# Gathered rows of an expert block asked for ahead, their transposes tied behind the queued unit, four row tiles

## The chip, the cores and the metric

The kernel runs on one core of a Trainium2 chip. The metric is the device time of one execution in microseconds (us). Of the core's engines, TensorE (PE) multiplies and transposes, VectorE (DVE) and ScalarE (ACT) copy and combine, GpSimd (POOL) issues the indirect transfers (gathers and scatters by a list of rows), and SyncE (SP) issues the plain ones. Each engine has a queue of its own and works through it in order.

## The reference

Attention with a block-wise causal mask, an MLP with a squared ReLU on its output, and a mixture of eight experts of which each token takes one:

```python
x = attention(q, k, v)                    # 4 x 8 heads x 576 x 64 -> x: 2304 tokens x 512
h = x @ w_in                              # 512 -> 2048
r = np.maximum(h, 0.0)
x = (r * r) @ w_out                       # 2048 -> 512
logits = x @ w_gate + modality_bias[modality_id]
e_idx = np.argmax(logits, axis=1)         # one of 8 experts
gate_w = softmax(logits)[arange(N), e_idx]
for e in range(8):
    mask = e_idx == e
    h = np.maximum(x[mask] @ w1[e], 0.0)  # 512 -> 1024
    out[mask] = gate_w[mask, None] * (h @ w2[e])
```

## The kernel before, in words

The tokens are worked in nine blocks of 256 (`BT`). Attention of later tokens runs interleaved with the MLP of earlier ones; the last MLP block, number 8, runs with no attention beside it (L873 to L886). An MLP or expert block is a list of *units* (`ffn_units`, L468): a unit f multiplies the block's transposed input, split in a high and a low part, by 128 columns of the first weight (twelve matmuls, L493 to L495, called U here), ScalarE and VectorE make gh and gl of the result (L506 to L512), and then the second matmuls of the unit before are done (L483 to L485, six for a block of 256 rows, nine for 352). An MLP block has 16 units, an expert block eight.

After each MLP block `route` (L570) writes its rows to x2d in HBM, computes the expert of each token, and scatters the token numbers into lists, one per expert (lst, L623 on POOL; the positions come from VectorE's L621). The rows of an expert block are then fetched by such a list: `load_list` (L655) loads 256 or 352 entries on SP, and `gather_block` (L666) takes the rows in tiles of 128 with an indirect DMA on POOL (L677), transposes each tile on PE (four transposes, L683, into a bank of tag s, of which there are two), and makes the high part on ScalarE (L685) and the low part on VectorE (L686).

Two experts with the most tokens after block 5 are worked as fixed blocks: the first two blocks of the first expert ("early", 256 rows each), then `blocks` (L888): its blocks of 352, 352, and four of the second expert (352, 352, 256, 256 rows). The early blocks' gathers are asked for at unit 10 of MLP block 8 (L882); the next ones at unit 6 of the second early block (L898), with the list three units before (L896), and then at unit 1 of each block for the block after it (L907). `expert_steps` (L796) splits the next expert's weights on ScalarE and VectorE (L193 to L197) beside the units; their loads (L186) are on SP. `expert_finish` (L689) scales the result and scatters it to out (L698, POOL).

What sets the order: the program is built with a scheduler that orders each engine's instructions by a simulated timeline. Code may run ahead of what was written before it, up to its data; `tc.issue_after` ties instructions behind a given one. So the place of a transpose in PE's queue is where the scheduler expects its rows to be there, and PE waits if they are not.

Of the kernel before, what the change touches and what calls it, by code (L numbers as in the profile page):

```python
# [10 lines left out]
F32 = mybir.dt.float32  # L11
# [9 lines left out]
P = 128  # L21
B, H, S, HD = 4, 8, 576, 64
N = B * S
D = H * HD
FF = 2048
E, FE = 8, 1024
KC = D // P
# [25 lines left out]
def tile_attention_mlp_moe(ctx: ExitStack, tc: tile.TileContext, qT2, kT2, v, w_in, w_out,  # L53
# [46 lines left out]
    def scratch(name):  # L100

        if late_pool:
            return late_pool[0].tile([P, D], F32, tag="xt", bufs=1, name=name)
        return apool.tile([P, S], F32, tag="p", bufs=6, name=name)[:, 0:D]
# [363 lines left out]
    def ffn_units(xh, xl, wa, wb, nf, square, finish, htag="h", bt=BT, last_blk=False):  # L468
# [18 lines left out]
        def unit(f):  # L487
# [4 lines left out]
            for k in range(KC):  # L492
                nc.tensor.matmul(hb[:, :bt], whk[:, k, :], xh[:, k, :], start=(k == 0), stop=False)  # L493
                nc.tensor.matmul(hb[:, :bt], whk[:, k, :], xl[:, k, :], start=False, stop=False)  # L494
                nc.tensor.matmul(hb[:, :bt], wlk[:, k, :], xh[:, k, :], start=False, stop=(k == KC - 1))  # L495
            if last_blk:
# [13 lines left out]
            else:  # L510
                act = nc.scalar.activation(out=gh, in_=hb[:, :bt], func=AF.Relu)  # L511
                dve = nc.vector.scalar_tensor_tensor(out=gl, in0=hb[:, :bt], scalar=0.0, in1=gh.bitcast(F32),  # L512
                                                     op0=ALU.max, op1=ALU.subtract)
            unit_ends[:] = [act, dve]
            pend.append((f, gh, gl))
# [149 lines left out]

    def gather_block(il, n):  # L666
        if n == BT:
            xh = work.tile([P, KC, BT], F32R, tag="xh", bufs=3, name="gxh")
            xl = work.tile([P, KC, BT], F32R, tag="xl", bufs=3, name="gxl")
        else:  # L670
            xh = late.tile([P, KC * LBT], F32R, tag="lxh", bufs=2, name="gxh")[:, 0:KC * n]
            xl = late.tile([P, KC * LBT], F32R, tag="lxl", bufs=2, name="gxl")[:, 0:KC * n]
            xh, xl = (x.rearrange("p (k c) -> p k c", k=KC) for x in (xh, xl))
        for t in range(-(-n // P)):
            w = min(P, n - t * P)
            g = late.tile([P, D], F32, tag="gat", bufs=3, name="gat")
            nc.gpsimd.indirect_dma_start(  # L677
                out=g[:w], out_offset=None, in_=x2d,
                in_offset=bass.IndirectOffsetOnAxis(ap=il[:w, t, 0:1], axis=0))
            tb = pbank("s", 2)  # L680
            tv = tb.rearrange("p (k q) -> p k q", k=KC)
            for k in range(KC):
                nc.tensor.transpose(tv[:, k, :w], g[:w, k * P:(k + 1) * P], ident[:w, :w])  # L683
            sl = slice(t * P, t * P + w)
            nc.scalar.copy(xh[:, :, sl], tv[:, :, :w])  # L685
            nc.vector.tensor_sub(xl[:, :, sl], tv[:, :, :w], xh[:, :, sl].bitcast(F32))  # L686
        return xh, xl
# [186 lines left out]
    early = []  # L874

    def get_early():
        for blk in range(2):
            il = load_list(rvs[0], blk, f"e{blk}")
            early.append((gather_block(il, BLKS[blk]), il))

    for f, u in enumerate(units):
        if f == NF1 // 2 + 2:  # L882
            get_early()
        if steps and f:
            steps.pop(0)()
        u()  # L886
# [4 lines left out]
    nxt = None  # L891
    for ei, ((xh, xl), il) in enumerate(early):
        for f, u in enumerate(ffn_units(xh, xl, *moe_w[0], NF2, False, expert_finish(il, BT), "pt")):
            if steps and (ei or f):
                steps.pop(0)()
            if ei and f == 3:  # L896
                lists += [load_list(rvs[0], blk, f"l0{blk}") for blk in (2, 3)]
            if ei and f == 6:  # L898
                nxt = gather_block(lists[0], BLKS[blocks[0][1]])
            u()  # L900
    lists += [load_list(loads_reg(1), blk, f"l1{blk}") for blk in ORDER]
    for gi, (i, blk) in enumerate(blocks):
        xh, xl = nxt
        n = BLKS[blk]
        units = ffn_units(xh, xl, *moe_w[i], NF2, False, expert_finish(lists[gi], n), "pt", n, gi == len(blocks) - 1)
        for f, u in enumerate(units):
            if f == 1 and gi + 1 < len(blocks):  # L907
                nxt = gather_block(lists[gi + 1], BLKS[blocks[gi + 1][1]])
            u()
# [87 lines left out]
```

## Time and profile before

| | |
|---|---|
| median of 3 runs | 892.41 us (890.43 to 898.46) |
| profiled execution | 891.78 us |
| its span, first to last instruction | 890.0 us |
| PE busy | 854.0 us (96%) |
| VectorE, ScalarE, GpSimd busy | 505.4, 400.3, 73.0 us |
| mean granted clock of PE | 0.988 |

The profile is of one execution. Busy times say what an engine did; for an engine that is nearly always busy, its waits and the stretches with a lower granted clock say where time is lost. MLP block 8 lies about from 600 to 650 us, the two early expert blocks to about 700 us, the six others after them.

### The profile page before, as it was taken

How to read it: one execution, taken by the hardware profiler on the slowest of the kernel's cores; microseconds unless marked ns; L12 is line 12 of the kernel's file. 1: busy time of each engine (PE TensorE's matmuls, PEld its weight loads, DVE VectorE, ACT ScalarE, POOL GpSimd, SP SyncE). 2: the span in 40 equal slices, each digit the busy share in tenths (PEclk: the TensorE clock that was granted, in tenths of full speed). 3: DMA queues.
4: the chain of work that ended last, by engine and by line, in shares of the span. 5: the costliest groups of instructions: out<-in, count | busy, mean ns of one | idle time of the engine just before them, and what ended most of it. 6: DMA issues, size and time to landing. Idle time of an engine off the chain costs nothing. (4 is left out here: it accounts for less than half of the span.)

```text
span 890.0 us, 16016 instructions
## 1 busy us (share of the span) xinstructions
PE 854.0 (96%) x5865; PEld 734.0 (82%) x5866; DVE 505.4 (57%) x1533; ACT 400.3 (45%) x1074; POOL 73.0 (8%) x174
## 2 busy tenths in 40 slices
PE   5799999999999999999999999999898999999997
PEld 4566778888988888888888888898787988888896
DVE  6989878968667647555837755348363312212221
ACT  6689888645555435444534434334232212112111
POOL 1000000001000000100000000100103202101011
PEclk9899999999999999999999999999998999999999
DMA  9983151221341210232211211420622101011000
GB/s 313 353 278 110 38 186 34 67 78 21 90 131 60 61 52 31 66 105 84 61 30 37 54 31 51 129 80 33 190 72 70 57 21 66 28 34 45 13 29 36
DMA packets 87922, 73.94 MB, mean 83 GB/s; under 512 B 14305, under 2 KB 75745, under 8 KB 87842
## 3 DMA queue, kind: packets, MB, share of 16 engines
q1 hardware_dynamic: 84194, 63.18, 23.9%
q0 software_dynamic: 3648, 9.72, 3.3%
q8 instruction: 47, 0.77, 0.4%
q14 instruction: 33, 0.27, 0.1%
HBM read 62.71 MB, written 10.42 MB: 82 GB/s over the span
## 5 line engine op out<-in xcount | busy, mean ns | idle before, releaser
L493 PE MATMUL h<-xh,w 128*128 128x256 f32 x512 | 149.7, 292 | 3.7 <-ACT r L506 3.7
L483 PE MATMUL acc<-w,gh 128*128 128x512 f32 x368 | 151.5, 412 | 0.4 <-ACT gh L508 0.4
L484 PE MATMUL acc<-w,gh 128*128 128x512 f32 x368 | 146.1, 397 | 0.0
L495 PE MATMUL h<-xh,w 128*128 128x256 f32 x512 | 145.9, 285 | 0.0
L494 PE MATMUL h<-xl,w 128*128 128x256 f32 x512 | 145.7, 285 | 0.0
L485 PE MATMUL acc<-w,gl 128*128 128x512 f32 x368 | 132.2, 401 | 0.0
L493 PEld LDWEIGHTS h<-xh,w 128*128 128x128 f32 x512 | 97.9, 191 | 8.8 <-ACT r L506 4.1
L506 ACT ACTIVATE r<-h 128x256 f32<-128x256 f32 x128 | 49.2, 384 | 121.2 <-PE h L495 119.2
L512 DVE SCALAR_TENSOR_TENSOR gl<-pt,gh 128x352 fp32r<-128x352 f32 (+1 forms) x56 | 26.9, 481 | 129.8 <-ACT gh L511 128.5
L494 PEld LDWEIGHTS h<-xl,w 128*128 128x128 f32 x512 | 98.0, 191 | 2.9 <-issue 0.2
L507 DVE TENSOR_TENSOR r<-r 128x256 f32<-128x256 f32 x128 | 53.9, 421 | 79.9 <-ACT r L506 79.2
L495 PEld LDWEIGHTS h<-xh,w 128*128 128x128 f32 x512 | 98.0, 191 | 0.4 <-issue 0.2
L511 ACT ACTIVATE gh<-pt 128x352 fp32r<-128x352 f32 (+1 forms) x56 | 24.1, 430 | 154.0 <-PE pt L495 145.8
L485 PEld LDWEIGHTS acc<-w,gl 128*128 128x128 f32 x368 | 67.6, 189 | 15.6 <-issue 1.5
L483 PEld LDWEIGHTS acc<-w,gh 128*128 128x128 f32 x368 | 70.2, 191 | 10.9 <-issue 1.5
L493 PE MATMUL pt<-gxh,w 128*128 128x256 f32 (+1 forms) x256 | 78.6, 307 | 0.0
L495 PE MATMUL pt<-gxh,w 128*128 128x256 f32 (+1 forms) x256 | 77.8, 304 | 0.0
L494 PE MATMUL pt<-gxl,w 128*128 128x256 f32 (+1 forms) x256 | 77.6, 303 | 0.0
L484 PEld LDWEIGHTS acc<-w,gh 128*128 128x128 f32 x368 | 70.3, 191 | 8.3
L508 ACT CAST gh<-r 128x256 fp32r<-128x256 f32 x128 | 52.0, 406 | 48.2 <-DVE r L507 48.2
L509 DVE TENSOR_TENSOR gl<-r,gh 128x256 fp32r<-128x256 f32 x128 | 53.7, 419 | 26.6 <-ACT gh L508 23.7
L340 ACT ACTIVATE p<-s,nmx 128x384 f32<-128x384 f32 (+2 forms) x96 | 56.2, 588 | 22.3 <-DVE nmx L335 13.4
(188 smaller groups left out, 1626.8 us busy)
## 6 DMA issues: line engine op xcount, KB each, us to landing
w<-w_in SPq DMA_DIRECT2D x16, 512.0 KB
w<-w_out SPq DMA_DIRECT2D x16, 512.0 KB
wraw<-w SPq DMA_DIRECT2D x32, 256.0 KB
v<-v SPq DMA_DIRECT2D x28, 256.0 KB
kraw<-kT SPq DMA_DIRECT2D x24, 288.0 KB
qraw<-qT SPq DMA_DIRECT2D x48, 128.0 KB
x2d<-x SPq DMA_DIRECT2D x18, 256.0 KB
v<-v SPq DMA_DIRECT2D x12, 192.0 KB
```

The costliest lines, as they stand in the source:

```text
L340: nc.scalar.activation(out=pb[:, c0:c0 + nv], in_=banks[i][:, :nv], func=AF.Exp, bias=nmx[:, 0:1], accum_out=sm[:, i:i + 1])
L483: nc.tensor.matmul(acc[t][:n], gh[:, sl], wh, start=(f == 0), stop=False)
L484: nc.tensor.matmul(acc[t][:n], gh[:, sl], wl, start=False, stop=False)
L485: return nc.tensor.matmul(acc[t][:n], gl[:, sl], wh, start=False, stop=(f == nf - 1))
L493: nc.tensor.matmul(hb[:, :bt], whk[:, k, :], xh[:, k, :], start=(k == 0), stop=False)
L494: nc.tensor.matmul(hb[:, :bt], whk[:, k, :], xl[:, k, :], start=False, stop=False)
L495: nc.tensor.matmul(hb[:, :bt], wlk[:, k, :], xh[:, k, :], start=False, stop=(k == KC - 1))
L506: nc.scalar.activation(out=r, in_=hb[:, :bt], func=AF.Relu)
L507: nc.vector.tensor_mul(r, r, r)
L508: act = nc.scalar.copy(gh, r)
L509: dve = nc.vector.tensor_sub(gl, r, gh.bitcast(F32))
L512: dve = nc.vector.scalar_tensor_tensor(out=gl, in0=hb[:, :bt], scalar=0.0, in1=gh.bitcast(F32), op0=ALU.max, op1=ALU.subtract)
```

## The change

`gather_block` is cut in two. `gather_rows` issues the indirect DMAs of a block and returns the row tiles; `turn_block` makes the transposes and the copies. The tag gat has four buffers instead of three, and `route`'s scratch tiles (xt, before a tag with one buffer) take theirs from the same tag. `turn_block` runs inside `tc.issue_after(unit_ends[2].ins)`, where the new third entry of `unit_ends` is the last matmul U of the unit that was queued last. Early blocks: rows are asked for at unit 10 as before, the turns are called ahead of unit 15 and of the step after it, so they come behind U of unit 14 and 15. Expert blocks: for the first, list and rows at unit 2 of the second early block, the turn at unit 6; for the others, rows at unit 1 and the turn at unit 4 of the block before.

```diff
     def scratch(name):
         if late_pool:
-            return late_pool[0].tile([P, D], F32, tag="xt", bufs=1, name=name)
+            return late_pool[0].tile([P, D], F32, tag="gat", bufs=4, name=name)
...
-                nc.tensor.matmul(hb[:, :bt], wlk[:, k, :], xh[:, k, :], start=False, stop=(k == KC - 1))
+                pe = nc.tensor.matmul(hb[:, :bt], wlk[:, k, :], xh[:, k, :], start=False, stop=(k == KC - 1))
...
-            unit_ends[:] = [act, dve]
+            unit_ends[:] = [act, dve, pe]
...
-    def gather_block(il, n):
+    def gather_rows(il, n):
+        res = []
+        for t in range(-(-n // P)):
+            w = min(P, n - t * P)
+            g = late.tile([P, D], F32, tag="gat", bufs=4, name="gat")
+            nc.gpsimd.indirect_dma_start(
+                out=g[:w], out_offset=None, in_=x2d,
+                in_offset=bass.IndirectOffsetOnAxis(ap=il[:w, t, 0:1], axis=0))
+            res.append(g)
+        return res
+
+    def turn_block(rows, n):
...
-        for t in range(-(-n // P)):
-            w = min(P, n - t * P)
-            g = late.tile([P, D], F32, tag="gat", bufs=3, name="gat")
-            nc.gpsimd.indirect_dma_start(
...
+        with tc.issue_after(unit_ends[2].ins):
+            for t, g in enumerate(rows):
+                w = min(P, n - t * P)
+                tv = pbank("s", 2).rearrange("p (k q) -> p k q", k=KC)
+                for k in range(KC):
+                    nc.tensor.transpose(tv[:, k, :w], g[:w, k * P:(k + 1) * P], ident[:w, :w])
+                sl = slice(t * P, t * P + w)
+                nc.scalar.copy(xh[:, :, sl], tv[:, :, :w])
+                nc.vector.tensor_sub(xl[:, :, sl], tv[:, :, :w], xh[:, :, sl].bitcast(F32))
         return xh, xl
...
     for f, u in enumerate(units):
         if f == NF1 // 2 + 2:
-            get_early()
+            for blk in range(2):
+                il = load_list(rvs[0], blk, f"e{blk}")
+                early.append([il, gather_rows(il, BLKS[blk])])
+        if f >= NF1 - 1:
+            early[f - NF1 + 1].append(turn_block(early[f - NF1 + 1][1], BT))
...
-            if ei and f == 3:
+            if ei and f == 2:
                 lists += [load_list(rvs[0], blk, f"l0{blk}") for blk in (2, 3)]
+                rows = gather_rows(lists[0], BLKS[blocks[0][1]])
             if ei and f == 6:
-                nxt = gather_block(lists[0], BLKS[blocks[0][1]])
+                nxt = turn_block(rows, BLKS[blocks[0][1]])
...
-            if f == 1 and gi + 1 < len(blocks):
-                nxt = gather_block(lists[gi + 1], BLKS[blocks[gi + 1][1]])
+            if f == 1 and more:
+                rows = gather_rows(lists[gi + 1], BLKS[blocks[gi + 1][1]])
+            if f == 4 and more:
+                nxt = turn_block(rows, BLKS[blocks[gi + 1][1]])
```

In the new program the copies are L694 (ScalarE) and L695 (VectorE), the transposes L692, the gathers L672, the scatters to out L707.

The first place is the end of MLP block 8. On PE before, the first tile's transposes stand behind the second matmuls of unit 10, ahead of U of unit 12 (L493 on); the other three tiles' stand a unit apart behind them:

```order
L484 MATMUL acc<-w,gh 128x512
L485 MATMUL acc<-w,gl 128x512 x2
L683 MATMUL s<-ident,gat 128x128 x4
L493 MATMUL h<-xh_6464,w 128x256
L494 MATMUL h<-xl_6465,w 128x256
L495 MATMUL h<-xh_6464,w 128x256
```

On PE now, both tiles of the first early block stand behind U of unit 14:

```order
L493 MATMUL h<-xh_6464,w 128x256
L494 MATMUL h<-xl_6465,w 128x256
L495 MATMUL h<-xh_6464,w 128x256
L692 MATMUL s<-ident,gat 128x128 x8
L483 MATMUL acc<-w,gh 128x512
L484 MATMUL acc<-w,gh 128x512
L483 MATMUL acc<-w,gh 128x512
```

The move shows in units on ScalarE, where a unit of block 8 is one L506 and one L508. Before, at the end of the block (the last row is the copy of the block's result):

```order
L508 CAST gh<-r 128x256
L685 CAST gxh<-s 128x4x128
L506 ACTIVATE r<-h 128x256
L508 CAST gh<-r 128x256
L685 CAST gxh<-s 128x4x128
L506 ACTIVATE r<-h 128x256
L508 CAST gh<-r 128x256
L685 CAST gxh<-s 128x4x128
L506 ACTIVATE r<-h 128x256
L508 CAST gh<-r 128x256
L685 CAST gxh<-s 128x4x128
```

And now, up to the copy of the block's result:

```order
L506 ACTIVATE r<-h 128x256
L508 CAST gh<-r 128x256
L506 ACTIVATE r<-h 128x256
L694 CAST gxh<-s 128x4x128 x2
L508 CAST gh<-r 128x256
L506 ACTIVATE r<-h 128x256
L508 CAST gh<-r 128x256
L694 CAST gxh<-s 128x4x128 x2
L835 COPY x_8479<-acc 128x512
```

The four copies stood behind one unit each; now they stand in pairs, the first ahead of L508 of unit 14. VectorE's L695 stand in the same way ahead of its L509. Besides, VectorE's L621 (the positions of block 7's tokens) stands behind six L507 of block 8, where it stood behind seven.

The second place is the two early expert blocks. On ScalarE before, from the result of the first early block on (a unit of 256 rows is one L511):

```order
L695 ACTIVATE y<-acc,il 128x512
L511 ACTIVATE gh<-pt 128x256
L685 CAST gxh<-s 128x4x128
L511 ACTIVATE gh<-pt 128x256 x2
L685 CAST gxh<-s 128x4x128
L511 ACTIVATE gh<-pt 128x256 x2
L685 CAST gxh<-s 128x4x96
```

And now:

```order
L704 ACTIVATE y<-acc,il 128x512
L511 ACTIVATE gh<-pt 128x256 x5
L694 CAST gxh<-s 128x4x128 x2
L511 ACTIVATE gh<-pt 128x256
L694 CAST gxh<-s 128x4x96
L511 ACTIVATE gh<-pt 128x256
```

The first tile's copy, and its transposes on PE, stand four units later. On PE before, six transposes stand behind U of unit 1 of the second early block and the seventh a unit later; now eight stand about U of unit 5.

The third place is POOL from the last scatter of a list on. Before:

```order
L623 DMA lst<-pay,pos 22528x2 x2
L677 DMA gat<-x2d,il 128x512 x2
L677 DMA gat<-x2d,il 96x512
L698 DMA out<-y,il 2304x512
L677 DMA gat<-x2d,il 128x512
L698 DMA out<-y,il 2304x512
L677 DMA gat<-x2d,il 128x512
L677 DMA gat<-x2d,il 96x512
```

And now:

```order
L623 DMA lst<-pay,pos 22528x2 x2
L672 DMA gat<-x2d,il 128x512 x2
L672 DMA gat<-x2d,il 96x512
L672 DMA gat<-x2d,il 128x512
L707 DMA out<-y,il 2304x512 x2
L672 DMA gat<-x2d,il 128x512
L672 DMA gat<-x2d,il 96x512
```

The first tile of the block after the next one stands ahead of the first scatter to out, which stood ahead of it. SP's order is the same as before.

## Rows read from the trace of the kernel before

**Rows 1.** The page's first part: busy us, share of span, instructions.

```profile
PE 854.0 (96%) x5865; PEld 734.0 (82%) x5866; DVE 505.4 (57%) x1533; ACT 400.3 (45%) x1074; POOL 73.0 (8%) x174
```

**Rows 2.** PE's waits, 600 to 890 us: waited for, us, times, longest.

```profile
PE s L683 <- DMA gat<-x2d,il: 6.4, 2, 4.0
PE pt L581 <- ACT x L826: 0.4, 1, 0.4
```

**Rows 3.** Windows: busy us of each engine, then clock, DMA share, GB/s.

```profile
620.00:628.76 8.76, 8.76 (x56) 7.69 (x55) 3.09 (x7) 2.64 (x7) 1.28 (x2) 1.00 0.04 1
628.76:637.19 8.43, 4.42 (x21) 4.08 (x21) 1.37 (x3) 1.11 (x3) 3.51 (x4) 0.80 1.00 323
664.00:668.00 4.00, 4.00 (x26) 3.56 (x25) 3.82 (x16) 1.78 (x4) 1.18 (x1) 1.00 0.01 0
680.68:683.00 2.32, 1.73 (x7) 1.33 (x8) 0.55 (x1) 0.58 (x1) 1.74 (x2) 0.50 0.85 245
683.00:687.30 4.30, 4.30 (x16) 3.72 (x15) 0.14 (x1) 0.00 (x0) 1.29 (x2) 0.50 0.32 99
690.00:715.00 25.00, 25.00 (x157) 22.80 (x156) 7.07 (x14) 6.19 (x14) 6.77 (x7) 1.00 0.20 61
```

**Rows 4.** Timeline of PE, block 8: start, us, operation, [idle before, releaser].

```profile
625.47 0.63 PE L485 MATMUL acc<-w,gl 128*128 128x512 f32 x2
628.29 0.63 PE L485 MATMUL acc<-w,gl 128*128 128x512 f32 x2
632.94 1.12 PE L683 MATMUL s<-ident,gat 128*128 128x128 f32 x4 [4.01 <-DMA gat<-x2d,il]
637.19 0.63 PE L485 MATMUL acc<-w,gl 128*128 128x512 f32 x2
...
643.72 0.63 PE L485 MATMUL acc<-w,gl 128*128 128x512 f32 x2
644.19 0.60 PE L683 MATMUL s<-ident,gat 128*128 128x128 f32 x4
646.98 0.63 PE L485 MATMUL acc<-w,gl 128*128 128x512 f32 x2
```

**Rows 5.** Timeline of PE, second early expert block.

```profile
676.28 0.63 PE L485 MATMUL acc<-w,gl 128*128 128x512 f32 x2
...
680.68 1.12 PE L683 MATMUL s<-ident,gat 128*128 128x128 f32 x4 [2.35 <-DMA gat<-x2d,il]
682.38 0.69 PE L683 MATMUL s<-ident,gat 128*128 128x128 f32 x2 [0.58 <-issue]
...
688.64 0.70 PE L485 MATMUL acc<-w,gl 128*128 128x512 f32 x2
```

**Rows 6.** Timeline of POOL: gathers (L677) and scatters of lists (L623).

```profile
628.44 0.98 POOL L677 DMA_INDIRECT gat<-x2d,il  x1 [5.09 <-DMA il<-lst]
629.72 0.95 POOL L677 DMA_INDIRECT gat<-x2d,il  x1 [0.30 <-issue]
...
634.33 0.94 POOL L677 DMA_INDIRECT gat<-x2d,il  x1 [2.39 <-PE s L683]
665.95 1.18 POOL L623 DMA_INDIRECT lst<-pay,pos  x1 [30.68 <-DVE pos L621]
670.36 0.97 POOL L623 DMA_INDIRECT lst<-pay,pos  x1 [3.23 <-DMA lst<-pay,pos]
677.16 0.98 POOL L677 DMA_INDIRECT gat<-x2d,il  x1 [5.83 <-DMA il<-lst]
```

**Rows 7.** Timeline of SP: the second expert's weight loads, 256 KB each.

```profile
627.62 8.51 SPq L186 DMA_DIRECT2D wraw<-w  x12
```

**Rows 8.** Timelines of ScalarE and VectorE: evacuation and copies in block 8.

```profile
644.82 0.59 ACT L685 CAST gxh<-s 128x512 fp32r<-128x512 f32 x1 [0.49 <-PE s L683]
644.37 0.42 DVE L509 TENSOR_TENSOR gl<-r,gh 128x256 fp32r<-128x256 f32 x1 [0.47 <-ACT gh L508]
645.44 0.69 DVE L686 TENSOR_TENSOR gxl<-s,gxh 128x512 fp32r<-128x512 f32 x1 [0.65 <-ACT gxh L685]
```

More of the change, by code (lines that the diff above doesn't have):

```diff
@@ L673, in gather_block @@
             xh, xl = (x.rearrange("p (k c) -> p k c", k=KC) for x in (xh, xl))
-        for t in range(-(-n // P)):
-            w = min(P, n - t * P)
-            g = late.tile([P, D], F32, tag="gat", bufs=3, name="gat")
-            nc.gpsimd.indirect_dma_start(
[L678 to L686, printed above, removed]
+        with tc.issue_after(unit_ends[2].ins):
[7 more added lines that the diff above has]
+                nc.vector.tensor_sub(xl[:, :, sl], tv[:, :, :w], xh[:, :, sl].bitcast(F32))
         return xh, xl
@@ L874, in tile_attention_mlp_moe @@
     early = []
[L876 to L879, printed above, removed]
     for f, u in enumerate(units):
         if f == NF1 // 2 + 2:
-            get_early()
+            for blk in range(2):
[3 more added lines that the diff above has]
+            early[f - NF1 + 1].append(turn_block(early[f - NF1 + 1][1], BT))
         if steps and f:
@@ L891, in tile_attention_mlp_moe @@
     nxt = None
-    for ei, ((xh, xl), il) in enumerate(early):
+    for ei, (il, _, (xh, xl)) in enumerate(early):
         for f, u in enumerate(ffn_units(xh, xl, *moe_w[0], NF2, False, expert_finish(il, BT), "pt")):
@@ L904, in tile_attention_mlp_moe @@
         n = BLKS[blk]
-        units = ffn_units(xh, xl, *moe_w[i], NF2, False, expert_finish(lists[gi], n), "pt", n, gi == len(blocks) - 1)
+        more = gi + 1 < len(blocks)
+        units = ffn_units(xh, xl, *moe_w[i], NF2, False, expert_finish(lists[gi], n), "pt", n, not more)
         for f, u in enumerate(units):
-            if f == 1 and gi + 1 < len(blocks):
-                nxt = gather_block(lists[gi + 1], BLKS[blocks[gi + 1][1]])
+            if f == 1 and more:
+                rows = gather_rows(lists[gi + 1], BLKS[blocks[gi + 1][1]])
+            if f == 4 and more:
+                nxt = turn_block(rows, BLKS[blocks[gi + 1][1]])
             u()
```

## The prediction

> **What bounds the kernel now.** The page's first part says that TensorE (PE) is busy 96% of the span [rows 1], so the other engines matter only where PE waits for them. I read PE's waits next. From 600 us to the end, where the whole change lies, PE waits 6.4 us for gathered rows (tile gat), 0.58 us at the same place without a named releaser, and at most 0.4 us for anything else [rows 2, 5]. So there are two holes, and both stand ahead of transposes of gathered rows. The windows show that the holes cost more than their idle time: the granted clock is 1.00 before the first and 0.80 from its start to its end, and 0.50 (the 1.2 GHz level) from the end of the second until 687.30; from 690 on it is 1.00 again and PE is busy the whole time [rows 3]. The timeline gives the price of each hole.
>
> Hole 1 is in block 8 of the MLP. A unit with nothing beside it takes 628.29 - 625.47 = 2.82 us from one L485 to the next; a unit with four transposes takes 646.98 - 643.72 = 3.26, so four transposes cost 0.44, one 0.11 [rows 4]. The unit with the hole holds exactly one unit's work and four transposes, and takes 637.19 - 628.29 = 8.90. Lost: 8.90 - 3.26 = 5.64 us, of which 4.01 are idle and the other 1.63 the slow clock after it.
>
> Hole 2 is in the second early expert block. From the L485 at 676.28 to that at 688.64 stand two units and seven transposes, 2 x 2.82 + 7 x 0.11 = 6.41; they take 12.36 [rows 5]. Lost: 5.95 us, 2.35 + 0.58 = 2.93 idle and 3.02 slow clock.
>
> Both have one cause: PE runs its queue in order, the scheduler put the transposes right where it expected the rows, and the chain scatter of positions, list load, gather came later than it expected. On POOL the gather waits for the list (5.09 and 5.83 us), and its rows land 632.94 - 628.44 = 4.50 and 680.68 - 677.16 = 3.52 us after the gather starts [rows 4 to 6].
>
> **Part by part.**
>
> *Early turn (hole 1).* The gathers stay where they are on POOL; the first tiles' transposes move on PE from ahead of units 12 and 13 to behind U of unit 14, those of the other two to behind U of unit 15. PE reaches the old place at 628.29 + 0.47 = 628.76, the 0.47 being 644.19 - 643.72 [rows 4]. Without a hole it gets to the end of unit 14 after two units and the half unit of U (taken as 1.41): 628.76 + 5.64 + 1.41 = 635.8. The first tile was there at 632.94. The second is asked for 1.3 us later (629.72 - 628.44, a gather and the 0.30 between two); at the same landing time it is there at 634.2, 1.6 us early. The second pair is wanted 0.88 (eight transposes) + 2.82 later, at 639.5. The fourth gather waited 2.39 us for a buffer [rows 6]; with four buffers it starts three steps after the first, at 632.3, and lands at 636.8. Besides, the positions stand one unit earlier in VectorE's order (six L507 of block 8 ahead of L621 instead of seven), so that the whole chain may start up to 2.82 us sooner; I take 0 of it for the sum. The hole goes: -5.64. Bound on the other side: twelve weight loads start at 627.62 on SP [rows 7] and fill the DMA engines at 323 GB/s [rows 3]; 12 x 256 KB, 3.1 MB, at that rate last until about 637.4. Were the first two tiles served only after them, their 0.5 MB would be there at about 637.4 + 1.6 = 639.0, 3.2 us late. The first tile landed in the midst of these loads, which speaks against it.
>
> *Expert turn (hole 2).* The list is asked for at f = 2 instead of 3, but the load waits for the last scatter (670.36 on POOL) either way, so nothing is gained there. All of this moves with PE: 5.64 us earlier, the gather starts at 671.5, and its tiles land at about 675.0, 676.3 and 677.6. PE ended the unit ahead of the old transposes at 680.68 - 2.35 = 678.33 [rows 5]; now 672.7, and the new place is four units further, 672.7 + 4 x 2.82 = 684.0. Margin 7 to 9 us; the chain would have to be twice as long to bring a wait back. -5.95. The gain holds also if hole 1 stays, as chain and PE then move together.
>
> *Added wait: copies in lumps.* Two tiles' transposes now stand together, and so do their copies. Behind unit 14 ScalarE does two L694 ahead of that unit's L508, VectorE two L695 ahead of its L509. Queued behind them is the unit's gh and gl, which PE needs for its second matmuls. From the end of U (T): the first copy starts when four transposes are done, 0.44 + (644.82 - 644.19 - 0.44) = T + 0.63; ScalarE is done at T + 0.63 + 2 x 0.59 = T + 1.81, VectorE, which starts 645.44 - 644.82 = 0.62 after it, at T + 1.25 + 2 x 0.69 = T + 2.63, and L509 at T + 3.05 [rows 8]. PE wants it after eight transposes, two halves of a unit and three transposes: 0.88 + 2.82 + 0.33 = T + 4.0. Cost 0; the cover is 0.95 us. Without it PE would wait at most the lump, 2 x (0.59 + 0.69) = 2.56 us.
>
> *Number of transposes, spread.* The same instructions as before, only in larger groups; I take 0.11 apiece either way: 0. *Four buffers, the shared tag with route's xt:* the second xt no longer waits for the first; PE had no wait over 0.4 us there, so 0 to -0.4, I take 0. *POOL:* the scatters of the first expert block stand behind one gather more (1.3 us). That is when y's buffers come free; the next y is a block of eight units later: 0.
>
> *A rule that speaks against asking early.* The row first: on POOL the gather or scatter instruction took 0.94 to 0.98 us, and 1.18 in the stretch where VectorE is busy 3.82 of 4 us, mostly with splits [rows 3, 6]: 0.21 more. Four gathers under splits would be 0.84 us later, which the 1.6 us of hole 1 cover: 0 in the sum. The Trainium skill says more (page "SBUF — State Buffer", section "A bandwidth-pool intuition that's wrong (but worth ruling out)"): GpSimd cannot write a DMA's descriptors until VectorE's copy releases the port they share, and its example grows from 620 to 3100 ns. By that ratio, an estimate, four gathers of 0.97 would be done 15.5 us later, PE would wait some 14 us for them in hole 1, and the sum would be about 895 instead of 880. The 1.18 row speaks for the smaller price.
>
> **Sum.** The profiled execution took 891.78 us (span 890.0 and 1.78 around it), 0.63 under the median of the runs shown, 892.41. 891.78 - 5.64 - 5.95 = **880.2 us**. A measurement of this kernel can tell about 1%, 8.9 us, from no change; the forecast is 12.2 below the median.
>
> **Rivals.**
>
> *One hole comes back.* Hole 1, if the gathers are served behind the weight loads: 3.2 us late, and an idle of 2.35 cost 3.02 of slow clock in hole 2, so the whole 5.6 again: 891.78 - 5.95 = 885.8. Or hole 2, if the list comes late by another wait (SP's queue): 891.78 - 5.64 = 886.1. For it: the margin of hole 1 is only 1.6 us. Against: the positions come sooner, and PE's order has 7 us for hole 2.
>
> *It doesn't do what it says.* The scheduler could have kept the transposes where they were: 891.8. The order of the built program shows the move, so this needs both chains to be slower than in the trace by their margins and the old holes together.
>
> *GpSimd is held by VectorE.* If VectorE's copies hold the gathers' instructions, hole 1 opens again from the point at which four of them are held for 1.6 us together; the row gives 0.84, and in VectorE's order the splits end ahead of the gathers. Held so far that hole 1 is whole: 885.8. The Trainium skill's page named above states such a hold.
>
> *The copies' lump is not covered, lightly.* At the end of block 8 only: one or two waits of at most 2.56, and the clock stays up or falls once: 882 to 885.
>
> *The copies' lump becomes the bound (slower).* There are eight such turns. If each held ScalarE and VectorE for 2.56 us ahead of a unit's gh and gl, that is 20.5 us, and if each dragged the clock as the holes did, at least 1.63 apiece, 13 us more: 880.2 + 33.5 = 913.7. It decides from the point at which the copies end later than the unit's gl is wanted: 0.9 us more at block 8, in the expert blocks about a unit. For it: all copies are in lumps now. Against: in the expert blocks they stand behind a unit's gh in ScalarE's order, and the engines are idle most of the time there (7.07 and 6.19 us of 25) [rows 3].
>
> **Chances.** Forecast, both holes gone, 878.4 to 882.0: 0.72. One hole back: 0.10. No effect: 0.03. GpSimd held: 0.02. Light lump: 0.08. Slower: 0.05. The range goes from 878.4 (the sum less 1.35, by which the fastest run lies below the profiled one, and less the 0.4 at L581) to 886.7 (886.1 and the 0.63 of the median); outside lie the slower case and the empty one, 0.08, and a run's own scatter. Faster by over 1% needs 883.5: the forecast and half of the light lump, 0.76. Within 1%: 0.19. Slower: 0.05.
>
> **What would show it.** In PE's waits after 600 us no row with gat, or one under 1 us; granted clock 1.00 in every window from 600 to 875; the unit behind unit 12 2.82 us long; the gathers on POOL in a row of four without a wait for PE's transposes; the last instruction some 11.6 us earlier. Step 1 is wrong if PE waits for gat about 7 us after the old place; step 2 if it does so in the second early block; the copies are wrong if PE waits for gh or gl behind unit 14. The prediction as a whole fails if PE's work between the holes got longer, or if time is lost after 690, where nothing was idle before.

## The result

The changed kernel takes 880.92 us (median of 6 runs, 878.07 to 883.33), the kernel before 892.37 beside it: a ratio of 0.9864 (95% interval 0.9838 to 0.989). The forecast was 880.2 us.

Both holes are gone. The page's first part after the change, then PE's waits from 600 us to the end (what is waited for, us, times, longest), and the busy time of the engines in windows (PE, weight loads, VectorE, ScalarE, GpSimd; then granted clock, DMA share, GB/s):

```profile
PE 851.0 (97%) x5865; PEld 732.1 (83%) x5866; DVE 504.8 (57%) x1533; ACT 399.7 (45%) x1074; POOL 73.4 (8%) x174
```

```profile
PE pt L581 <- ACT x L835: 0.4, 1, 0.4
PE h L493 <- ACT r L506: 0.3, 1, 0.3
PE pv L586 <- ACT xt L264: 0.2, 1, 0.2
```

```profile
620.00:640.00 20.00, 19.70 (x130) 17.68 (x129) 7.68 (x19) 6.11 (x16) 4.90 (x5) 1.00 0.60 185
660.00:690.00 30.00, 30.00 (x201) 27.30 (x200) 14.50 (x39) 7.58 (x17) 8.41 (x9) 1.00 0.20 52
```

The row with gat, 6.4 us before [rows 2], has no successor; the windows that stood at 0.80 and 0.50 [rows 3] are at 1.00. New is a wait of 0.30 us for r (L506).

Two marks make the executions comparable: the first transposes of route of block 7 and of block 8 (L581). PE's timeline before, then after (start, us, operation, [idle before, releaser]):

```profile
597.20 1.03 PE L581 MATMUL pt<-ident,x 128*128 128x128 f32 x8
649.75 1.09 PE L581 MATMUL pt<-ident,x 128*128 128x128 f32 x8 [0.44 <-ACT x L826]
```

```profile
600.09 1.04 PE L581 MATMUL pt<-ident,x 128*128 128x128 f32 x8
...
639.31 1.03 PE L692 MATMUL s<-ident,gat 128*128 128x128 f32 x8
...
642.99 0.49 PE L692 MATMUL s<-ident,gat 128*128 128x128 f32 x3
...
644.71 0.72 PE L485 MATMUL acc<-w,gl 128*128 128x512 f32 x2
...
647.27 1.09 PE L581 MATMUL pt<-ident,x 128*128 128x128 f32 x8 [0.44 <-ACT x L835]
...
686.96 0.49 PE L692 MATMUL s<-ident,gat 128*128 128x128 f32 x3
```

From the first mark to the second (stretch A, with the place of hole 1) it was 52.55 us and is 47.18. From the second mark to the end of the span (stretch B, with hole 2) it was 890.0 - 649.75 = 240.25 and is 881.1 - 647.27 = 233.83. Gained: 5.37 and 6.42, together 11.79. The part ahead of the marks, which the change doesn't touch, was 2.89 us longer in this execution; it differs that much between executions of one kernel (in a second profile of the changed kernel the first mark stands at 593.67, not 600.09). Stretches A and B are therefore the finer measure below: where nothing in a stretch was changed, A came out between 46.59 and 47.18 and B between 233.65 and 234.00.

POOL after the change, the four gathers in a row and the list of the next ones; then how long all gathers took to land, and SP's weight loads:

```profile
622.53 0.96 POOL L623 DMA_INDIRECT lst<-pay,pos  x1 [3.36 <-DMA lst<-pay,pos]
628.60 0.98 POOL L672 DMA_INDIRECT gat<-x2d,il  x1 [5.12 <-DMA il<-lst]
629.89 0.96 POOL L672 DMA_INDIRECT gat<-x2d,il  x1 [0.30 <-issue]
631.15 1.05 POOL L672 DMA_INDIRECT gat<-x2d,il  x1 [0.30 <-issue]
632.51 0.95 POOL L672 DMA_INDIRECT gat<-x2d,il  x1 [0.31 <-issue]
663.46 1.19 POOL L623 DMA_INDIRECT lst<-pay,pos  x1 [30.00 <-DVE pos L621]
667.66 1.06 POOL L623 DMA_INDIRECT lst<-pay,pos  x1 [3.01 <-DMA lst<-pay,pos]
675.26 0.98 POOL L672 DMA_INDIRECT gat<-x2d,il  x1 [6.54 <-DMA il<-lst]
```

```profile
DMA to landing us min/median/max: 3.2/3.4/7.2
```

```profile
627.77 8.67 SPq L186 DMA_DIRECT2D wraw<-w  x12
```

The fourth gather no longer waits for PE [rows 6]. From the first mark the first gather starts at 628.60 - 600.09 = 28.51, where it started at 628.44 - 597.20 = 31.24: 2.73 sooner.

ScalarE and VectorE behind unit 14, where the copies now come in pairs:

```profile
639.94 1.07 ACT L694 CAST gxh<-s 128x512 fp32r<-128x512 f32 x2
640.90 0.42 ACT L508 CAST gh<-r 128x256 fp32r<-128x256 f32 x1
```

```profile
640.56 1.29 DVE L695 TENSOR_TENSOR gxl<-s,gxh 128x512 fp32r<-128x512 f32 x2 [0.15 <-ACT gxh L694]
641.77 0.42 DVE L509 TENSOR_TENSOR gl<-r,gh 128x256 fp32r<-128x256 f32 x1
```

### The profile page after: what moved, and what is told of

Its sections match the earlier page's. It is cut to its first block, busy times and chain, and to the rows that moved or that the text cites. A ratio compares the mean times of both kernels' runs of the same rounds, so it can differ in the third digit from the quotient of the medians.

```text
span 881.1 us, 16022 instructions
## 1 busy us (share of the span) xinstructions
PE 851.0 (97%) x5865; PEld 732.1 (83%) x5866; DVE 504.8 (57%) x1533; ACT 399.7 (45%) x1074; POOL 73.4 (8%) x174
## 5 line engine op out<-in xcount | busy, mean ns | idle before, releaser
L493 PE MATMUL h<-xh,w 128*128 128x256 f32 x512 | 149.9, 293 | 4.6 <-ACT r L506 4.6
L493 PEld LDWEIGHTS h<-xh,w 128*128 128x128 f32 x512 | 97.8, 191 | 10.6 <-ACT r L506 5.9
L506 ACT ACTIVATE r<-h 128x256 f32<-128x256 f32 x128 | 49.3, 385 | 124.5 <-PE h L495 121.1
L507 DVE TENSOR_TENSOR r<-r 128x256 f32<-128x256 f32 x128 | 54.0, 422 | 84.9 <-ACT r L506 84.2
L511 ACT ACTIVATE gh<-pt 128x352 fp32r<-128x352 f32 (+1 forms) x56 | 24.1, 431 | 134.7 <-PE pt L495 134.7
L493 PE MATMUL pt<-gxh,w 128*128 128x256 f32 (+1 forms) x256 | 78.1, 305 | 0.0
L508 ACT CAST gh<-r 128x256 fp32r<-128x256 f32 x128 | 52.0, 406 | 47.6 <-DVE r L507 47.6
L509 DVE TENSOR_TENSOR gl<-r,gh 128x256 fp32r<-128x256 f32 x128 | 53.7, 419 | 25.9 <-ACT gh L508 23.1
```

The source lines that it names most:

```text
L506: nc.scalar.activation(out=r, in_=hb[:, :bt], func=AF.Relu)
L507: nc.vector.tensor_mul(r, r, r)
L508: act = nc.scalar.copy(gh, r)
L509: dve = nc.vector.tensor_sub(gl, r, gh.bitcast(F32))
```

## The experiments

Theory: a hole is PE's queue reaching transposes ahead of their rows; each hole is a cost of its own, idle time and slow clock, and goes away by putting the transposes behind enough queued units. Rivals: the gain comes from asking ahead or from the fourth buffer; the slow clock has another cause; the copies' lumps cost something.

All ratios are to the kernel before on the same chip, from 5 to 12 executions of each kernel; A and B are the stretches above, in us, of one execution, the profiled one. A and B of the kernel before are from the profile above.

| kernel | ratio (95% interval) | A | B |
|---|---|---|---|
| before | 1 | 52.55 | 240.25 |
| changed | 0.9864 (0.9838 to 0.989) | 47.18 | 233.83 |
| changed, again | 0.9853 (0.9819 to 0.9888) | 46.87 | 233.66 |
| early turns only | 0.9923 (0.9896 to 0.9949) | 46.59 | 238.43 |
| expert turns only | 0.9954 (0.993 to 0.9977) | 53.59 | 233.65 |
| untied | 0.9994 (0.9977 to 1.0011) | 54.00 | 239.16 |
| three row tiles | 0.9887 (0.986 to 0.9914) | 48.55 | 233.78 |
| turns 2 units sooner | 0.9885 (0.9858 to 0.9912) | 48.67 | 234.00 |
| turns 3 units sooner | 0.9918 (0.9889 to 0.9946) | 52.15 | 233.91 |
| the same, filled | 0.9907 (0.9881 to 0.9933) | 51.98 | 233.96 |
| turns one by one | 0.9925 (0.9897 to 0.9954) | 51.27 | 233.72 |
| the same, filled | 0.991 (0.9879 to 0.9941) | 49.96 | 233.73 |
| copies twice | 0.9901 (0.9868 to 0.9934) | 47.54 | 235.10 |
| copies four times | 1.0012 (0.999 to 1.0033) | 47.41 | 246.78 |

The changed kernel's repetition, the measure of the last group (turns one by one, with and without filling, and copies twice):

> The changed kernel itself, on the chip of the three other runs of this group, as their measure: a ratio to the kernel before of 0.986 as in its own measurement (0.9838 to 0.989), 47 to 48 us between the first transposes of the two routes, no wait for rows.

It held, but for A just under 47: a ratio of 0.9853, A 46.87, no wait for rows.

### One hole at a time

**Early turns only.** The expert blocks call the old gather_block again:

```diff
-            if ei and f == 2:
+            if ei and f == 3:
...
-                rows = gather_rows(lists[0], BLKS[blocks[0][1]])
             if ei and f == 6:
-                nxt = turn_block(rows, BLKS[blocks[0][1]])
+                nxt = gather_block(lists[0], BLKS[blocks[0][1]])
...
-                rows = gather_rows(lists[gi + 1], BLKS[blocks[gi + 1][1]])
-            if f == 4 and more:
-                nxt = turn_block(rows, BLKS[blocks[gi + 1][1]])
+                nxt = gather_block(lists[gi + 1], BLKS[blocks[gi + 1][1]])
```

> Only the early blocks' rows are asked for ahead and turned behind units 14 and 15; the expert blocks are gathered and turned as before the change, without a tie (four row tiles stay). In PE's order the first hole's transposes stand where the changed kernel has them, and the second hole's stand where they stood before: six transposes behind U of unit 1 of the second early block. Theory (each hole is a PE queue that reaches transposes ahead of their rows, and each costs its own 5.6 to 6.0 us, idle time and slow clock): hole 1 gone, hole 2 back with 2.9 us idle and a clock of 0.50 for some 3 us behind it; 880.9 + 5.95 = 886.9. Rival (the list chain of hole 2 runs sooner once hole 1 is gone, because the chain and PE are not moved by the same amount): hole 2 small, 881 to 884. Rival (the gain came from four buffers and the second xt): 881, no hole.

PE's timeline of this kernel:

```profile
668.29 0.63 PE L485 MATMUL acc<-w,gl 128*128 128x512 f32 x2
672.19 0.66 PE L714 MATMUL s<-ident,gat 128*128 128x128 f32 x4 [1.85 <-DMA gat<-x2d,il]
673.68 0.69 PE L714 MATMUL s<-ident,gat 128*128 128x128 f32 x2 [0.84 <-DMA gat<-x2d,il]
...
679.26 0.70 PE L485 MATMUL acc<-w,gl 128*128 128x512 f32 x2
```

Two units and seven transposes, 6.41 us, took 10.97: hole 2 is back with 2.69 idle and 1.87 of slow clock. A is as short as in the changed kernel. The theory holds; the size is smaller than expected.

**Expert turns only.** The early blocks call the old gather_block at unit 10:

```diff
...
-                early.append([il, gather_rows(il, BLKS[blk])])
-        if f >= NF1 - 1:
-            early[f - NF1 + 1].append(turn_block(early[f - NF1 + 1][1], BT))
+                early.append([il, None, gather_block(il, BLKS[blk])])
```

> Only the expert blocks (those behind the two early ones) are asked for ahead and turned behind a queued unit; the early blocks are gathered and turned as before the change, without a tie (four row tiles stay). In PE's order the first tile's transposes stand a unit earlier than before the change, ahead of U of unit 11, as the positions too stand a unit earlier in VectorE's order; the second hole's stand where the changed kernel has them. Theory (each hole by itself): hole 1 back, about 4 us idle and 1.6 of slow clock, hole 2 gone: 880.9 + 5.64 = 886.5, with PE's wait for gat at about 4 us, once. Rival (hole 1 is larger, because the rows now come while the second expert's weights load, and the third and fourth tile land 7 us behind their gathers as in the profile of the changed kernel): two or more waits for gat, 888 to 892.

PE's timeline:

```profile
621.75 0.63 PE L485 MATMUL acc<-w,gl 128*128 128x512 f32 x2
626.75 1.12 PE L714 MATMUL s<-ident,gat 128*128 128x128 f32 x4 [4.37 <-DMA gat<-x2d,il]
631.69 0.62 PE L485 MATMUL acc<-w,gl 128*128 128x512 f32 x2
```

A unit and four transposes, 3.26 us, took 9.94: 4.37 idle and 2.31 slow, one wait. Hole 1 is back, 6.7 us where 5.64 were forecast; hole 2 stays away (B as in the changed kernel). What the two halves gain alone, 0.0077 and 0.0046, sums to 0.0123 beside 0.0136, and each stretch is as short as in the changed kernel when only the other hole is back: the holes are independent, as far as these runs tell.

### What makes the gain

**Untied.** The rows are asked for ahead, four tiles, but the scheduler may place the transposes:

```diff
-        with tc.issue_after(unit_ends[2].ins):
+        with ExitStack():
```

> The changed kernel without its tie: rows are asked for at the same points, in four row tiles, but the transposes may be placed by the scheduler. In PE's order they go back to about where they stood before: first tile a unit earlier than before the change, the second hole's six behind U of unit 1 of the second early block. Theory (the gain is the place of the transposes in PE's queue; asking in the code ahead of it does nothing by itself, as the chain of list and gather was ready no sooner): both holes back, 880.9 + 5.6 + 5.95 = 892.4, PE's wait for gat 6 to 7 us. Rival (asking ahead and four tiles give the gain, the tie is only neat): 881 to 883, no wait for gat above 1 us.

PE's waits:

```profile
PE s L692 <- DMA gat<-x2d,il: 7.9, 3, 4.6
```

The whole gain is gone. Asking ahead in the code does nothing here. POOL's timelines show why: the first gather waits for its list in the kernel before (5.09 us [rows 6]), in the changed one (5.12 above) and without the tie (4.96), so it already starts as early as the list allows. The tie is what counts.

**Three row tiles**, and route's scratch back in its own buffer:

```diff
-            return late_pool[0].tile([P, D], F32, tag="gat", bufs=4, name=name)
+            return late_pool[0].tile([P, D], F32, tag="xt", bufs=1, name=name)
...
-            g = late.tile([P, D], F32, tag="gat", bufs=4, name="gat")
+            g = late.tile([P, D], F32, tag="gat", bufs=3, name="gat")
```

> The changed kernel with three row tiles and route's scratch back in its own single buffer. The positions stand a unit later in VectorE's order, as before the change, and the fourth gather has to wait for the first tile's transposes behind unit 14. Theory (the new place of the transposes has room for both): gathers about 2.8 us later than in the changed kernel, the first three at some 631.4, 632.7 and 634.0, there by 636 to 638 against 639.3 wanted; the fourth at about 640, there at 643.2 to 644.5 against 644.7 wanted: 881 to 882, no wait above 0.5 us. Rival (the fourth buffer was needed: rows take up to 7.2 us to land, the longest in the profile of the changed kernel): the fourth tile comes at 647, a wait of 2.5 us and slow clock of 1.6 to 3 us behind it: 885 to 886.

POOL and PE:

```profile
619.48 0.96 POOL L623 DMA_INDIRECT lst<-pay,pos  x1 [2.90 <-DMA lst<-pay,pos]
634.18 1.05 POOL L672 DMA_INDIRECT gat<-x2d,il  x1 [5.25 <-PE s L692]
```

```profile
594.67 1.03 PE L581 MATMUL pt<-ident,x 128*128 128x128 f32 x8
640.76 0.63 PE L692 MATMUL s<-ident,gat 128*128 128x128 f32 x4 [1.76 <-DMA gat<-x2d,il]
```

Between the two expectations: the fourth tile is late by 1.76 us, and A is 1.4 to 1.7 longer than in the changed kernel, so nothing but the wait is lost; a window around it (638 to 644 us) shows the clock at 1.00. The list's scatter starts 24.81 us behind the first mark, in the changed kernel 22.44, so the positions come a unit sooner with four tiles and the shared tag. The run takes back the fourth tile and the shared tag together and doesn't part them. The trace has the landing of each early gather of this kernel: 5.1, 6.4, 7.4 and 6.4 us after its start. The intervals of the ratios overlap, so the 1.5 us rest on the traces.

### How much room the new place has

**Two and three units sooner.** The edit for two; for three it has f + 3:

```diff
-        if f >= NF1 - 1:
-            early[f - NF1 + 1].append(turn_block(early[f - NF1 + 1][1], BT))
+        if NF1 - 1 <= f + 2 <= NF1:
+            early[f + 2 - NF1 + 1].append(turn_block(early[f + 2 - NF1 + 1][1], BT))
```

> The changed kernel with the early turns two units sooner: behind U of units 12 and 13 instead of 14 and 15. PE reaches the first place 2 x 2.82 = 5.64 us sooner, at 639.31 - 5.64 = 633.67 in the time of the changed kernel's profile; its gathers start at 628.60, 629.89, 631.15 and 632.51, the third and fourth land at about 638.4 and 639.6 there. First tile by the two runs with a hole here (gather to transposes 5.04 us in the run with the expert blocks alone, 5.23 without the tie): about 633.7, just in time. Theory (rows asked for under the second expert's weight loads take longer than the 4.5 us of the forecast, 6 to 7 us from the second on, so the margin of the new place was not 1.6 us but smaller, and two units sooner is too soon): the second tile at about 636.4 against 634.1 wanted, a wait of about 2.3 us, and up to 1 us more ahead of the second pair: 880.9 + 2.5 = 883.4, up to 886 if the clock falls behind it. Rival (4.5 us for each tile, as forecast: the second at 634.4, the fourth at 637.0): no wait above 0.4 us, 881.

> The same, three units sooner: the first tile right behind U of unit 11, at 639.31 - 8.46 = 630.85, the second half a unit further, the others a unit apart. Theory: the first tile, there at about 633.7, is waited for 2.9 us, the second (636.4) about 0.9 us more, and the clock falls as it did in the old hole, for another 1.6 to 2.5 us: 880.9 + 3.8 + 2 = 886.7. Rival (4.5 us for each tile): one wait of 2.3 us, 883 to 885.

Two units sooner, PE and POOL:

```profile
598.23 1.04 PE L581 MATMUL pt<-ident,x 128*128 128x128 f32 x8
631.23 0.60 PE L692 MATMUL s<-ident,gat 128*128 128x128 f32 x4
633.36 0.66 PE L692 MATMUL s<-ident,gat 128*128 128x128 f32 x4 [1.53 <-DMA gat<-x2d,il]
```

```profile
627.96 0.96 POOL L672 DMA_INDIRECT gat<-x2d,il  x1 [0.30 <-issue]
```

The first tile is in time, the second comes 633.36 - 627.96 = 5.40 us after its gather and is waited for, the second pair is not late: between theory (2.3) and rival (none), nearer to the theory. Behind the first mark it lands at 35.13; the changed kernel wants it at 639.31 + 0.44 - 600.09 = 39.66, so its margin there is 4.5 us by this run (the 0.44 are the first tile's four transposes).

Three units sooner, PE, and a window behind the wait:

```profile
633.30 0.66 PE L692 MATMUL s<-ident,gat 128*128 128x128 f32 x4 [3.44 <-DMA gat<-x2d,il]
```

```profile
633.30:639.50 6.20, 6.20 (x30) 5.44 (x31) 1.91 (x4) 1.86 (x4) 0.00 (x0) 0.72 1.07 351
```

One wait of 3.44, 5.25 us after the gather's start (628.05); A is 5.0 to 5.3 longer than in the changed kernel's two profiles, so 1.5 to 1.8 us went to the clock. The hole returns as forecast, the second wait of the theory does not.

### Is the slow clock a price of its own?

**Filled.** 28 transposes of the identity, 0.11 us each, ahead of the first early tile, with the turns three units sooner:

```diff
...
+                for _ in range(fill if t == 0 else 0):
+                    nc.tensor.transpose(tv[:, 0, :], ident, ident)
...
```

> The same as three units sooner, with 28 more transposes of the identity (0.11 us each in the trace, 3.1 us together) on PE ahead of the first pair's: 9 right behind U of unit 11, 19 behind the second matmuls that follow; both tiles' transposes come behind those. The added work is not used. It fills the time in which PE would stand idle. PE then wants the rows at 630.85 + 1.0 + 1.4 + 2.1 = 635.3. Theory (the slow clock behind a hole comes from PE standing idle, and is a cost of its own): no idle time above 1 us, granted clock 1.00 throughout, so that only the 3.1 us and up to 1 us of a wait for the second tile are lost: 880.9 + 3.1 + 0.5 = 884.5, some 2 us less than the kernel with the hole in the same place, though it does more work. Rival (the clock falls at this place for another reason, the weight loads that run then): it falls here too, and the time is 886 to 887.

The scheduler now put the second tile's transposes right behind the first's, and PE waited 1.77 us for that one (7.34 us after its gather), so A was as long as without the filling. The clock stayed at 1.00, but as a sum the run decides nothing. With each tile tied behind a unit of its own (turn_tile does for one tile what turn_block does for a block; its last argument is the number of added transposes), no second tile is in the way:

```diff
...
+        if NF1 - 4 <= f < NF1:
+            turn_tile(*early[(f - NF1 + 4) // 2][1:], f % 2, 28 if f == NF1 - 4 else 0)
```

> The changed kernel with its four early row tiles turned one at a time, behind U of units 11, 12, 13 and 14 (pairs behind 14 and 15 in the changed kernel); the rest as there. The control of the next run. The first tile's place is that of the kernel with the turns three units sooner, where PE waited 3.44 us and the clock fell; the others come late enough that only the first is waited for. Theory: one hole of 3.4 us with 1.5 to 2 us of slow clock behind it; from the first transposes of block 7's route to those of block 8's 47.2 - 0.3 + 3.4 + 1.5 = 51.8 us or more (47.2 in the changed kernel, where 0.3 are a wait for r), 885.6 in all.

> The same with 28 more transposes of the identity on PE ahead of the first tile's: 9 right behind U of unit 11, 19 behind the second matmuls that follow, 3.1 us (the added work is not used). PE comes to the first tile 4.5 us after U of unit 11 instead of at once, the row is there by then, and the second tile is wanted a unit later, so that this time no wait for a second tile takes the place of the first. Theory (the slow clock is a price of standing idle, apart from the idle time): no wait above 0.4 us, granted clock 1.00, the stretch 47.2 - 0.3 + 3.1 = 50.0 us, 1.8 us less than the control, and 884 in all, though it does 3.1 us more work. Rival (the clock falls at this place whatever PE does, because of the transfers or the place in the block): the clock falls to 0.75 or less, the stretch is 51.5 or more.

Without filling, PE's wait, and the window from 625 to 630; then the same window with filling:

```profile
626.03 1.12 PE L706 MATMUL s<-ident,gat 128*128 128x128 f32 x4 [2.86 <-DMA gat<-x2d,il]
```

```profile
625.00:630.00 5.00, 3.97 (x17) 3.51 (x18) 1.02 (x2) 0.89 (x2) 0.91 (x1) 0.66 1.04 343
```

```profile
625.00:630.00 5.00, 5.00 (x41) 4.69 (x40) 0.92 (x2) 0.79 (x2) 2.78 (x3) 1.00 1.02 345
```

Beside the changed kernel's 46.87 on this chip, A is 4.40 longer without filling (2.86 idle, 1.54 slow clock) and 3.09 longer with it, which is the added work and nothing else. The DMA engines are as full in both windows, so the transfers don't lower the clock; PE's standing idle does. The kernel with more work ends its stretch 1.3 us sooner. This rests on one execution of each; the whole times don't show it. The ratios, 0.9925 and 0.991, point the same way but their intervals overlap, and the medians, 881.01 without filling and 881.20 with it, don't differ.

### The copies' lumps

**Each copy four times, and twice.**

```diff
-                nc.scalar.copy(xh[:, :, sl], tv[:, :, :w])
-                nc.vector.tensor_sub(xl[:, :, sl], tv[:, :, :w], xh[:, :, sl].bitcast(F32))
+                for _ in range(4):
+                    nc.scalar.copy(xh[:, :, sl], tv[:, :, :w])
+                for _ in range(4):
+                    nc.vector.tensor_sub(xl[:, :, sl], tv[:, :, :w], xh[:, :, sl].bitcast(F32))
```

> The changed kernel with each copy of a turn (high part on ScalarE, low part on VectorE) done four times, the first three not used; a turn of two tiles then has 8 x 0.54 = 4.3 us on ScalarE and 8 x 0.65 = 5.2 us on VectorE instead of 1.07 and 1.29. Where they may, they stand apart: in block 8 ScalarE makes two of them, the gh of unit 14, five, then r of unit 15; VectorE makes gl of unit 14 ahead of all of them. The point from which lumps decide, by the changed kernel's profile: gl of unit 14 is ready at 642.19 and wanted at about 644.7, 2.5 us of cover. Theory (the lumps of the changed kernel are covered everywhere; four times the work breaks the cover at block 8, where r and gl of unit 15, the block's result and the first expert block's gxl stand behind it, and not in the expert blocks, where a unit is 2.8 to 3.9 us and both engines are idle most of the time): waits of PE of 2 to 4 us together at the end of block 8 and the start of the first expert block, 1.6 to 2.5 us of slow clock, 883 to 887. Rival (lumps bind at each of the eight turns): eight waits of at least 2 us, 897 or more. Rival (no effect): 881.

Four times: windows of all engines, POOL and PE in stretch B:

```profile
650.00:660.00 10.00, 10.00 (x65) 9.04 (x64) 10.00 (x26) 3.98 (x10) 0.00 (x0) 1.00 0.34 107
...
680.00:690.00 10.00, 7.06 (x47) 5.98 (x46) 0.85 (x2) 1.97 (x5) 4.48 (x5) 1.00 0.39 75
...
700.00:720.00 20.00, 17.48 (x85) 15.55 (x86) 4.69 (x9) 3.26 (x8) 2.46 (x4) 0.83 0.11 39
```

```profile
677.50 0.97 POOL L623 DMA_INDIRECT lst<-pay,pos  x1 [0.59 <-DMA lst<-pay,pos]
684.30 0.98 POOL L672 DMA_INDIRECT gat<-x2d,il  x1 [5.84 <-DMA il<-lst]
```

```profile
642.52 0.65 PE L581 MATMUL pt<-ident,x 128*128 128x128 f32 x4 [0.44 <-ACT x L837]
...
687.70 0.66 PE L692 MATMUL s<-ident,gat 128*128 128x128 f32 x4 [2.60 <-DMA gat<-x2d,il]
...
701.11 0.95 PE L493 MATMUL pt<-gxh,w 128*128 128x352 f32 x2 [2.10 <-ACT gxh L695]
703.48 0.66 PE L494 MATMUL pt<-gxl,w 128*128 128x352 f32 x1 [1.41 <-DVE gxl L697]
```

All expectations were wrong: some 13 us are lost, but neither at block 8 (A hardly moves) nor at each of the eight turns (the last wait lies at 703 us). VectorE, full with repeated copies and splits (10.00 of 10 us), makes the positions late; the first gather starts 684.30 - 642.52 = 41.78 behind the second mark, where it started at 675.26 - 647.27 = 27.99. PE wants the rows at 42.58 instead of 39.69. So the chain is 13.79 - 2.89 = 10.9 later against PE. In the changed kernel the rows land at about 675.26 + 3.4 = 678.7 and are wanted at 686.96, 8.3 later; 10.9 - 8.3 = 2.6 is the wait measured. Hole 2's wait for rows is back through another door. It is the smaller part of the 13 us: behind it the clock stays at 1.00 (680 to 690), and more is lost from 695 to 704 us, in the main where the first block of 352 rows starts and waits 2.10 and 1.41 for the high and low part that this very turn copies four times; there the clock falls (0.83 from 700 to 720). How much of that comes from the late rows and how much from the added copies, the run doesn't tell.

> The changed kernel with each copy of a turn done twice, the first not used (four times in the run before this one, where VectorE was busy 10.00 of 10 us behind block 8, the last scatter of the lists came 14.6 us later behind the route's first transposes than in the changed kernel, and PE waited 2.60 us for the rows in the second early block). Theory (the copies cost something only when they hold back the positions on VectorE by more than the 8.3 us between the rows' landing and PE's call for them): in VectorE's order the positions of block 8 stand as in the changed kernel, one copy of a turn more ahead of them; the scatter comes 1 to 3 us later, no wait for rows, at most 1 us of small waits at the end of block 8: 881 to 882.5, a ratio to the kernel before of 0.986 to 0.988. Rival (each doubled turn costs PE a wait for gh or gl): eight waits of 0.5 to 1.3 us, 885 to 891.

Twice: the scatter comes 661.39 - 640.70 = 20.69 behind the second mark (661.02 - 640.54 = 20.48 in the changed kernel beside it), PE has no wait for rows, and waits 0.54 for a gh at block 8 (638.60 us) and 1.05 for the gxl of the first block of 352 rows (691.63). A and B are 0.7 and 1.4 longer, the ratio somewhat worse than expected (0.9901). So the positions are not held back, as the theory said, and six of the eight turns cost nothing, against the rival; but of the two waits only the smaller is at the end of block 8, and the loss is twice the 1 us expected.

## Why the prediction was right, point by point

**Holes as bound: right.** Forecast 5.64 + 5.95 = 11.59, measured 11.79 between mark and end and 11.45 in the medians. Hole 1 gave 5.37, of which the new 0.30 wait for r must be added back (5.67); hole 2 gave 6.42. The gain is well above the 6.94 us of idle time in the forecast, so the slow clock's share (4.65) is saved too; that standing idle is what lowers the clock rests on the turns one by one, with and without filling.

**Early turn: the step held, its margin was mis-sized three times.** The landing was taken as 4.50 us for each tile. Where PE waited for a first tile it was 4.98 to 5.25 (one by one, expert only, untied, three units sooner), for second tiles 5.40 and 7.34, for a fourth 6.58, all under the weight loads. In the changed kernel itself the third and fourth tile landed 7.2 and 7.1 us after their gathers, at 638.4 and 639.6, about when the rival of rows served behind the loads had the first two there (639.0); in the runs where PE waited for those, they came sooner. The earlier positions, taken as 0, brought 2.73. And the new place was put up to 0.6 us too early behind the first mark (635.8 - 597.20 = 38.6; measured 39.22, in the second profile 38.9). Together the second tile has 2.6 to 4.5 us (three units sooner and filled 37.02, two units sooner 35.13, wanted 39.66) instead of 1.6, or 2.0 if the first tile's 0.44 is counted there too. With the landing alone corrected and the positions left where they were, it is there at 629.72 - 597.20 + 5.40 to 7.34 = 37.9 to 39.9: 1.7 us ahead of PE, or 0.2 behind it. The run with three row tiles has the positions about there: its second tile landed at 626.55 + 6.4 = 632.95, and PE called for it at 633.31 + 0.44 = 633.75, without a wait. So the step held by itself in that run, but with 0.8 us only. That the error in the landing (0.9 to 2.8 us) was met by one in the other direction (2.73) is luck.

**Expert turn: right.** Margin forecast 7 to 9 us, 8.3 by the rows, and confirmed by the 2.60 us wait when the chain came 10.9 later.

**Copies in lumps: cost 0, right; the cover was mis-sized.** L509 ends at 642.19, T + 2.88 with T = 639.31 (forecast T + 3.05). PE calls for gl at 644.71, T + 5.4 (forecast T + 4.0), because five more transposes and the gh matmuls stand ahead of it. 2.5 us of cover, not 0.95. The tightest place found is another: in the changed kernel the last low part for the first block of 352 rows ends at 694.94, and PE calls for it at 696.28, 1.3 us of cover where the forecast had about a unit, 2.82; with the copies done twice PE waits there. Four times the copies also hold back the positions behind them on VectorE; the rival of a late list named another wait for it, SP's queue.

**Four buffers: needed, as forecast; the shared tag was taken as 0.** Three tiles and a tag of its own for xt lose 1.4 to 1.7 us, through the fourth tile, whose gather the forecast had starting without a wait under the early turn. What the shared tag is worth alone no run shows, but the positions, 2.73 us sooner in the changed kernel, are hardly sooner without it (the list's scatter 24.81 us behind the first mark, 622.39 - 597.20 = 25.19 before). The spread of transposes, taken as 0: B is 4.6 to 4.8 longer in the early-only kernel, its hole 4.56, which leaves 0.0 to 0.2.

**GpSimd held by VectorE: not seen.** The four gathers took 0.98, 0.96, 1.05 and 0.95. The longest indirect issue of a list in any of these runs was

```profile
617.00 1.48 POOL L623 DMA_INDIRECT lst<-pay,pos  x1 [2.77 <-DMA lst<-pay,pos]
```

in the early-only kernel: 0.5 us above the usual 0.96, about as long as one of VectorE's instructions beside it (0.43 to 0.69). The Trainium skill (page "SBUF — State Buffer", section "A bandwidth-pool intuition that's wrong (but worth ruling out)") has 620 growing to 3100 ns; no run here shows such a step, and the 895 that the forecast scaled from it has no ground in these rows.

**A rival's price.** One hole back was put at 885.8 or 886.1. By ratio, hole 2 alone gives 0.9923 x 892.4 = 885.5, hole 1 alone 888.3 (886.1 to 890.3 by its interval): it cost 6.7 us in the expert-only profile against 5.64 in that of before, where the first tile landed 4.50 and not 5.04 us after its gather. Of the difference 0.36 us are idle and 0.68 slow clock.

## What to carry to other kernels

Where an in-order queue waits for a gather, look at where the transposes stand in it, not at where the gather is asked for: here the request was already as early as its list allowed, and tying the consumer behind queued work made the gain. Price such a hole as idle time plus the slow clock behind it, where the windows show one, and work out the margin of the new place from landings under the transfers that really run beside it. Then look at what else feeds the chain: an engine that is off the critical path, like VectorE with the positions here, brings the hole back once its backlog exceeds that margin.

## What was not expected of the hardware

Gathered rows that land 3.2 to 3.7 us after the gather's start behind 660 us (DMA share 0.20 in the window from 660 to 690) took 4.5 to 7.4 us while twelve 256 KB weight loads ran (DMA share 1.0, some 340 GB/s), and the later tiles of a group took longer than the first (5.1, then 6.4 and 7.4 with three row tiles).

Behind waits of 1.53, 1.76, 1.77 and 2.60 us the windows show a clock of 1.00; with 2.86, 3.44 and 4.01 us it was 0.66, 0.72 and 0.80 in the windows around. The length of one wait doesn't settle it: in hole 2 waits of 2.35 and 0.58 us, or of 1.85 and 0.84, were followed by 0.50. Extra work on PE in place of a wait kept the clock at 1.00 and lengthened the stretch by less than the wait did (3.09 us against 4.40).
